# A cross-network kernel: remainder loads re-queued between ScalarE and SyncE, bias copies on ScalarE, one block order

## The chip, the cores and the metric

The kernel runs on one core of a Trainium2 chip. The metric is the device time of one execution in microseconds (us); lower is better. A core has TensorE (PE, matrix products into PSUM), VectorE (DVE), ScalarE (ACT), GpSimd (POOL) and SyncE (SP). SyncE and ScalarE issue DMA transfers here, each on a queue of its own; an engine issues in program order.

## What is computed

Six cross layers (DCN v2) over 4096 rows of 416 features in bf16:

```python
B, F, D, L = 4096, 26, 16, 6          # Din = F * D = 416
def reference(x0, ws, bs):            # x0 [4096, 416], ws [6, 416, 416], bs [6, 416]
    x = x0
    for l in range(ws.shape[0]):
        x = x0 * (x @ ws[l] + bs[l]) + x
    return x
```

## The kernel before

**Layout.** x is kept transposed, features on partitions. The 416 features are three full blocks of 128 (XM, index m for output blocks and k for input blocks) and a remainder of 32. The batch is cut in two halves s = 0 and 1 of 2048 rows, each into four column groups of 512. The four groups of the remainder are stacked on the partitions of one tile XR (group g on partitions 32g to 32g+31), and XRx holds the same with the two 64-partition halves exchanged, so that a matmul can take a group from another row strip of the array. Layers 0 to 4 are computed in this layout; the last layer puts batch rows on partitions and ends in the stores.

**Loads.** Eight transposing DMAs of 512 batch rows each (`load_x0t`, line 77, all from SyncE) bring XM[0]; this text calls them loads 1 to 8. The remainder columns come as plain rows of 64 bytes into `xrem` (`load_xrem`, line 82), in four parts of 64 KB, two for each half of the batch: R0a and R0b (partitions 0:64 and 64:128 of the first half), R1a and R1b (second half). `x0_rem` (line 160) turns a part into XR with VectorE transposes (line 164) and copies (line 165, by ScalarE and VectorE), and then into XRx (line 167, VectorE). For the second half one call handles R1a and R1b together, so it needs both. Layer 0's weights, the biases (`bsb`, line 99) and the remainder rows of the weights (WR, line 100) are issued by ScalarE ahead of everything else.

**Queues before.** SyncE: load 1, load 2, R0a, loads 3 to 6, R1b, loads 7 and 8, then the other layers' weights and the rows of x0 for the last layer. ScalarE: layer 0's weights, biases, WR, three copies of WR rows (line 115), R0b, its share of R0a's copies, R1a. GpSimd: bias columns (lines 105 to 109), three copies of the bias rows to the other partition strips (line 111), then the WD copies (line 136). The bias rows on all strips are first read in the last layer (line 351).

**Layer 0** (`first_layer`, line 239) is written out by hand. TensorE runs warm-up matmuls, then, for the first half: a block of 18 full matmuls (line 246; three output blocks m, two column groups gl, three k each) in PSUM pairs `pa`; six row matmuls (line 254) that add the remainder's part from XR and XRx; a second block of 18 in `pb`; its rows. ScalarE (lines 189 and 172) and VectorE (line 190) take the results out of PSUM. The second half follows with a third block of 18 and its rows. Groups gl = 0 and 1 of the first block read loads 1 and 2, those of the second block loads 3 and 4, those of the third loads 5 and 6. The order of m and gl within a block is a literal list (line 258), which differs between the halves.

**PSUM.** PSUM is used as four pairs of banks, given out by `two_banks` in the order of line 142: the first half's `pa` has pairs 0, 1, 2, its `pb` pairs 3, 0, 2; the second half's `pa` has 1, 3, 0. A pair that is given out again must have been emptied.

Of the kernel before, what the change touches and what calls it, by code (L numbers as in the profile page):

```python
# [16 lines left out]
def kernel(  # L17
# [7 lines left out]
    nc = tc.nc  # L25
# [4 lines left out]
    R = D - NK * P  # L30
    assert R == 32 and B == 4096 and D == 416 and L >= 2
    NS = 2
    NG = 4
# [22 lines left out]
    bsb = const.tile([P, D], BF16)  # L56
# [12 lines left out]
    def col0(s, g):  # L69
        return SW * s + CW * g  # L70
# [4 lines left out]
    def load_x0t(s, g):  # L75
        c0 = col0(s, g)
        nc.sync.dma_start_transpose(out=XM[0][:, :, c0:c0 + CW], in_=x0[c0:c0 + CW, 0:NK * P])


    def load_xrem(eng, s, p0, p1):  # L80
        with nc.allow_non_contiguous_dma(reason="64B row segments"):
            eng.dma_start(xrem[s][p0:p1], x0[SW * s + 16 * p0:SW * s + 16 * p1, NK * P:D].rearrange("(p t) r -> p t r", t=16))
# [24 lines left out]
    for g in range(NG):  # L107
        nc.gpsimd.tensor_copy(bR[32 * g:32 * g + 32, :], bT[:, 4 * NK, 0:L])
    nc.gpsimd.tensor_scalar(out=bR[:, 0:1], in0=bR[:, 0:1], scalar1=1.0, scalar2=None, op0=ALU.add)
    for g in range(1, NG):  # L110
        nc.gpsimd.tensor_copy(bsb[32 * g:32 * g + 32, :], bsb[0:R, :])
    for g in range(1, NG):
        nc.vector.tensor_copy(WR[32 * g:32 * g + 32, 0, :], WR[0:32, 0, :])
    for g in range(1, NG):
        nc.scalar.copy(WR[32 * g:32 * g + 32, 1, :], WR[0:32, 1, :])
    load_x0t(0, 1)
    load_xrem(nc.sync, 0, 0, 64)
    load_xrem(nc.scalar, 0, 64, 128)
    load_x0t(0, 2)
    load_x0t(0, 3)  # L120
    load_x0t(1, 0)
    load_x0t(1, 1)
    load_xrem(nc.sync, 1, 64, 128)
    load_x0t(1, 2)
# [20 lines left out]
    def two_banks():  # L145
        n = turn[0]
        i = first_order[n] if n < len(first_order) else (2, 1, 0, 3)[(n - len(first_order)) % 4]
        turn[0] += 1
        return PS[:, 2 * i:2 * i + 2, :]
# [10 lines left out]
    def x0_rem(s, p0, p1, parts):  # L160
        XRv = XR[0][p0:p1, CW * s:CW * s + CW].rearrange("p (j t) -> p j t", t=16)
        n = 16 // len(parts)
        for a, copy in enumerate(parts):
            nc.vector.transpose(out=xrt[s][p0:p1, n * a:n * a + n, :], in_=xrem[s][p0:p1, n * a:n * a + n, :])  # L164
            copy(XRv[:, :, n * a:n * a + n], xrt[s][p0:p1, n * a:n * a + n, :].rearrange("p t j -> p j t"))
        for a in range(p0, p1, 64):
            nc.vector.tensor_copy(XRx[s][64 - a:128 - a, :], XR[0][a:a + 64, CW * s:CW * s + CW])


    def ew_copy(l, m, pt):  # L170
        t = tpool.tile([P, 2 * CW], BF16, name="t")
        nc.scalar.activation(t[:], pt.rearrange("p a b -> p (a b)"), ACT.Identity, bias=bM[:, m, l:l + 1], scale=1.0)  # L172
        return t[:]

    def ew_main(l, s, m, h, pt, cur, nxt):
        c0 = col0(s, 2 * h)
        t = ew_copy(l, m, pt)
        x0c = XM[0][:, m, c0:c0 + 2 * CW]
        if l == 0:
            nc.vector.tensor_tensor(out=nxt[:, m, c0:c0 + 2 * CW], in0=t, in1=x0c, op=ALU.mult)  # L180
            return
        nc.vector.tensor_tensor(out=t, in0=t, in1=x0c, op=ALU.mult)  # L182
        nc.vector.tensor_tensor(out=nxt[:, m, c0:c0 + 2 * CW], in0=t, in1=cur[:, m, c0:c0 + 2 * CW], op=ALU.add)  # L183


    def split_first(s, m, h, pt, nxt):
        c0 = col0(s, 2 * h)
        t = tpool.tile([P, 2 * CW], BF16, name="t")
        nc.scalar.activation(t[:, 0:CW], pt[:, 0, :], ACT.Identity, bias=bM[:, m, 0:1], scale=1.0)  # L189
        nc.vector.scalar_tensor_tensor(out=nxt[:, m, c0 + CW:c0 + 2 * CW], in0=pt[:, 1, :], scalar=bM[:, m, 0:1],  # L190
                                       in1=XM[0][:, m, c0 + CW:c0 + 2 * CW], op0=ALU.add, op1=ALU.mult)
        return lambda: nc.vector.tensor_tensor(out=nxt[:, m, c0:c0 + CW], in0=t[:, 0:CW], in1=XM[0][:, m, c0:c0 + CW], op=ALU.mult)
# [19 lines left out]
    def mm_row(l, s, m, pts, curR, first, last):  # L212
        for g in range(NG):
            nc.tensor.matmul(pts[g // 2][:, g % 2, :], lhsT=WR[32 * g:32 * g + 32, l, 128 * m:128 * m + 128],  # L214
                             rhs=curR[32 * g:32 * g + 32, CW * s:CW * s + CW],
                             start=first, stop=last, tile_position=(32 * g, 0), skip_group_check=True)
# [11 lines left out]
    def new_pts():  # L228
        return [two_banks() for h in range(2)]
# [9 lines left out]
    def first_layer(s):  # L239
        cur, nxt = XM[0], XM[1]  # L240

        def full(pt, m, h, gl, first, last):
            c0 = col0(s, 2 * h + gl)
            for k in range(NK):
                for q0, q1 in [(32 * q, 32 * q + 32) for q in range(4)] if s == 1 and h == 1 else ((0, P),):
                    nc.tensor.matmul(pt[q0:q1, gl, :], lhsT=WM[:, 0, k, 128 * m + q0:128 * m + q1], rhs=cur[:, k, c0:c0 + CW],  # L246
                                     start=(first and k == 0), stop=(last and k == NK - 1),
                                     tile_position=(0, q0) if s == 1 and h == 1 else None, skip_group_check=True)

        def row(pt, m, h, swapped, first):  # L250
            for gl in range(2):
                r0 = 32 * ((2 * h + gl + 2 * swapped) % 4)
                src = XRx[s][r0:r0 + 32, :] if swapped else XR[0][r0:r0 + 32, CW * s:CW * s + CW]
                nc.tensor.matmul(pt[:, gl, :], lhsT=WR[r0:r0 + 32, 0, 128 * m:128 * m + 128], rhs=src,  # L254
                                 start=first, stop=(not first), tile_position=(r0, 0), skip_group_check=True)

        pa = [two_banks() for m in range(NK)]
        for m, gl in ((0, 0), (1, 0), (2, 0), (0, 1), (1, 1), (2, 1)) if s == 0 else ((0, 0), (1, 0), (0, 1), (1, 1), (2, 0), (2, 1)):
            full(pa[m], m, 0, gl, True, False)
        pb = [two_banks()]  # L260
        row(pa[0], 0, 0, 0, False)
        if s == 1:
            row(pb[0], 0, 1, 0, True)
        row(pa[2], 2, 0, 0, False)
        row(pa[1], 1, 0, 1, False)
        if s == 0:
            closing = [split_first(s, 0, 0, pa[0], nxt)]
            closing.append(split_first(s, 2, 0, pa[2], nxt))
            t1 = ew_copy(0, 1, pa[1])
            for close in closing:  # L270
                close()
            x0_rem(0, 64, 128, (nc.scalar.copy, nc.vector.tensor_copy))
            nc.vector.tensor_tensor(out=nxt[:, 1, 0:2 * CW], in0=t1, in1=XM[0][:, 1, 0:2 * CW], op=ALU.mult)
            pb += [two_banks() for m in range(1, NK)]
            for m, gl in ((0, 0), (1, 0), (2, 0), (0, 1), (1, 1), (2, 1)):
                full(pb[m], m, 1, gl, True, False)
            row(pb[0], 0, 1, 0, False)
            row(pb[1], 1, 1, 0, False)
            row(pb[2], 2, 1, 1, False)
            split_first(s, 0, 1, pb[0], nxt)()  # L280
            x0_rem(1, 0, 128, (nc.vector.tensor_copy,))
            for m in range(1, NK):
                ew_main(0, s, m, 1, pb[m], cur, nxt)
            return None
        split_first(s, 0, 0, pa[0], nxt)()
        for m in (2, 1):
            ew_main(0, s, m, 0, pa[m], cur, nxt)
        full(pb[0], 0, 1, 0, False, False)
        rem_first(0)
        pb += [two_banks() for m in range(1, NK)]  # L290
        full(pb[1], 1, 1, 0, True, False)
        full(pb[0], 0, 1, 1, False, True)
        ew_main(0, s, 0, 1, pb[0], cur, nxt)
        full(pb[1], 1, 1, 1, True, False)
        for gl in range(2):
            full(pb[2], 2, 1, gl, True, False)
        row(pb[1], 1, 1, 0, False)
        row(pb[2], 2, 1, 1, False)
        pt = new_pts()
        mm_row(1, 0, 0, pt, XR[1], True, False)  # L300
        for m in range(1, NK):
            ew_main(0, s, m, 1, pb[m], cur, nxt)
        return pt

    x0_rem(0, 0, 64, (nc.scalar.copy, nc.vector.tensor_copy))
    load_xrem(nc.scalar, 1, 0, 64)

    def rem_pair(l, cur, curR, nxtR, feeds_last):
        pr2 = two_banks()
# [9 lines left out]
    def rem_first(s):  # L319
        pr = two_banks()  # L320
        mm_rem(0, s, pr[:, 0, :], XM[0], XR[0])
        ew_rem(0, s, pr[:, 0, :], XR[0], XR[1])
# [31 lines left out]
    first_layer(0)  # L354
    fill_wd(1, L)
    opened = first_layer(1)


    for l in range(1, LL):
# [6 lines left out]
        def close(t):  # L366
            s, m = t
            for h in range(2):
                ew_main(l, s, m, h, pts[t][h], cur, nxt)
            if feeds_last:  # L370
                xl_dmat(s, m, nxt)
# [116 lines left out]
```

## Time and profile before

| | us |
|---|---|
| median of 3 runs | 130.61 (130.51 to 131.05) |
| the profiled execution | 130.41 |
| its span (first to last instruction) | 128.6 |
| granted TensorE clock, mean | 0.998 |

Busy tenths of the span in 40 slices of 3.2 us, and what the DMA engines did:

```profile
PE   6998999999999999999999999999999999999950
DVE  3358769558697989898989898989898999999990
ACT  2357468693966684966684966584967586676860
POOL 4282000400000000000000000000000050000000
DMA  3999999999970000000000000000599999999563
```

Each digit is the busy share of a slice in tenths. Loads fill the first 37 us; then the DMA engines rest until the last layer. The waits on TensorE by what ended them, in total, times and longest, hold few rows beyond the issue of weights:

```profile
PE PS L153 <- DVE warm L87: 1.0, 1, 1.0
PE PS L246 <- DMA XM<-in_x_dram: 0.5, 2, 0.4
```

The first is the wait for the warm-up's operand at the very start. Matmuls are pipelined, so a gap between the starts of two matmuls that is shorter than one matmul's length does not appear as a wait; such gaps are found by comparing how long equal blocks take.

### The profile page before, as it was taken

How to read it: one execution, taken by the hardware profiler on the slowest of the kernel's cores; microseconds unless marked ns; L12 is line 12 of the kernel's file. 1: busy time of each engine (PE TensorE's matmuls, PEld its weight loads, DVE VectorE, ACT ScalarE, POOL GpSimd, SP SyncE). 2: the span in 40 equal slices, each digit the busy share in tenths (PEclk: the TensorE clock that was granted, in tenths of full speed). 3: DMA queues.
4: the chain of work that ended last, by engine and by line, in shares of the span. 5: the costliest groups of instructions: out<-in, count | busy, mean ns of one | idle time of the engine just before them, and what ended most of it. 6: DMA issues, size and time to landing. Idle time of an engine off the chain costs nothing. (4 is left out here: it accounts for less than half of the span.)

```text
span 128.6 us, 4040 instructions
## 1 busy us (share of the span) xinstructions
PE 122.5 (95%) x1731; PEld 54.9 (43%) x1731; DVE 105.4 (82%) x192; ACT 84.9 (66%) x97; POOL 8.9 (7%) x29
## 2 busy tenths in 40 slices
PE   6998999999999999999999999999999999999950
PEld 3343344444544443554443444443444454454420
DVE  3358769558697989898989898989898999999990
ACT  2357468693966684966684966584967586676860
POOL 4282000400000000000000000000000050000000
PEclk9999999999999999999999999999999999999999
DMA  3999999999970000000000000000599999999563
GB/s 97 259 178 211 189 208 260 262 329 337 333 219 9 3 0 5 0 5 0 5 0 5 0 5 0 0 5 0 54 200 192 123 165 211 77 344 285 178 208 102
DMA packets 41933, 16.28 MB, mean 127 GB/s; under 512 B 30838, under 2 KB 41916, under 8 KB 41916
## 3 DMA queue, kind: packets, MB, share of 16 engines
q1 hardware_dynamic: 39344, 15.53, 55.3%
q10 hardware_dynamic: 2572, 0.51, 2.2%
q8 instruction: 13, 0.21, 0.7%
q14 instruction: 4, 0.03, 0.1%
HBM read 6.07 MB, written 3.41 MB: 74 GB/s over the span
## 5 line engine op out<-in xcount | busy, mean ns | idle before, releaser
L172 ACT ACTIVATE t<-PS,bM 128x1024 bf16<-128x1024 f32 x56 | 58.1, 1114 | 24.0 <-PE PS L214 22.8
L208 PE MATMUL PS<-XM,WM 128*32 128x512 bf16 x1152 | 65.2, 379 | 0.0
L208 PEld LDWEIGHTS <-WM 128*32 128x32 bf16 x1152 | 29.8, 97 | 33.8 <-issue 5.1
L182 DVE TENSOR_TENSOR t<-t,XM 128x1024 bf16<-128x1024 bf16 x48 | 33.2, 691 | 5.4 <-ACT t L172 5.3
L183 DVE TENSOR_TENSOR XM<-t,XM 128x1024 bf16<-128x1024 bf16 x48 | 33.5, 699 | 2.9
L337 PE MATMUL PS<-WM,XM 128*128 128x416 bf16 x96 | 17.9, 340 | 0.0
L246 PE MATMUL PS<-XM,WM 128*32 128x512 bf16 (+1 forms) x126 | 16.6, 379 | 0.6 <-DMA XM<-in_x_dram 0.5
L405 ACT CAST t<-PS 128x832 bf16<-128x832 f32 x12 | 10.1, 854 | 4.2 <-PE PS L337 2.9
L337 PEld LDWEIGHTS <-XM 128*128 128x128 bf16 x96 | 8.9, 98 | 8.6 <-issue 2.1
L246 PEld LDWEIGHTS <-WM 128*32 128x32 bf16 (+1 forms) x126 | 7.2, 97 | 9.6 <-issue 2.6
L225 PE MATMUL PS<-XM,WM 128*32 128x512 bf16 x120 | 8.2, 379 | 0.0
L407 DVE TENSOR_TENSOR o<-t,XLrows 128x832 bf16<-128x832 bf16 x12 | 7.1, 592 | 0.5
L214 PE MATMUL PS<-XR,WR 32*128 32x512 bf16 x96 | 7.5, 379 | 0.0
L406 DVE TENSOR_TENSOR t<-t,X0rows 128x832 bf16<-128x832 bf16 x12 | 7.0, 585 | 0.0
L180 DVE TENSOR_TENSOR XM<-t,XM 128x1024 bf16<-128x1024 bf16 x7 | 4.8, 691 | 2.8 <-ACT t L172 2.7
L316 POOL COPY XLrows<-scrR 128x512 bf16<-128x512 bf16 x2 | 1.6, 809 | 77.3 <-DMA scrR<-XR 77.3
L196 ACT ACTIVATE t<-PS,bR 128x512 bf16<-128x512 f32 x10 | 6.8, 696 | 0.0
L189 ACT ACTIVATE t<-PS,bM 128x512 bf16<-128x512 f32 x4 | 2.6, 685 | 4.7 <-PE PS L254 4.7
L153 PE MATMUL PS<-warm 128*128 128x512 bf16 (+2 forms) x13 | 4.5, 527 | 1.0 <-DVE warm L87 1.0
L418 ACT CAST t<-PS 128x416 bf16<-128x416 f32 x8 | 4.0, 505 | 1.0 <-PE PS L337 0.6
L225 PEld LDWEIGHTS <-WM 128*32 128x32 bf16 x120 | 3.2, 97 | 3.1
L164 DVE STREAM_TRANSPOSE xrt<-xrem 64x256 bf16<-64x256 bf16 (+1 forms) x5 | 2.2, 477 | 2.3 <-DMA xrem<-in_x_dram 2.3
(45 smaller groups left out, 55.3 us busy)
## 6 DMA issues: line engine op xcount, KB each, us to landing
X0rows<-in_x_dram SPq DMA_DIRECT2D x6, 416.0 KB, 7.7
WM<-in_ws_dram SPq DMA_DIRECT2D x5, 312.0 KB, 5.5
out_dram<-o SPq DMA_DIRECT2D x3, 416.0 KB, 4.3
out_dram<-o SPq DMA_DIRECT2D x6, 208.0 KB, 2.1
X0rows<-in_x_dram SPq DMA_DIRECT2D x1, 832.0 KB, 9.6
out_dram<-o SPq DMA_DIRECT2D x8, 104.0 KB, 1.7
WR<-in_ws_dram SPq DMA_DIRECT2D x4, 104.0 KB, 4.8
WM<-in_ws_dram ACTq DMA_DIRECT2D x1, 312.0 KB, 3.4
```

Of the source, the lines that this page charges most:

```text
L172: nc.scalar.activation(t[:], pt.rearrange("p a b -> p (a b)"), ACT.Identity, bias=bM[:, m, l:l + 1], scale=1.0)
L182: nc.vector.tensor_tensor(out=t, in0=t, in1=x0c, op=ALU.mult)
L183: nc.vector.tensor_tensor(out=nxt[:, m, c0:c0 + 2 * CW], in0=t, in1=cur[:, m, c0:c0 + 2 * CW], op=ALU.add)
L196: nc.scalar.activation(tr[:, 0:CW], pr, ACT.Identity, bias=bR[:, l:l + 1], scale=1.0)
L208: nc.tensor.matmul(pts[g // 2][32 * q:32 * q + 32, g % 2, :], lhsT=WM[:, l, k, 128 * m + 32 * q:128 * m + 32 * q + 32], rhs=cur[:, k, c0:c ...
L214: nc.tensor.matmul(pts[g // 2][:, g % 2, :], lhsT=WR[32 * g:32 * g + 32, l, 128 * m:128 * m + 128], rhs=curR[32 * g:32 * g + 32, CW * s:CW ...
L225: nc.tensor.matmul(pr[32 * g:32 * g + 32, :], lhsT=WM[:, l, k, NK * P:D], rhs=cur[:, k, c0:c0 + CW], start=False, stop=(k == NK - 1), tile ...
L246: nc.tensor.matmul(pt[q0:q1, gl, :], lhsT=WM[:, 0, k, 128 * m + q0:128 * m + q1], rhs=cur[:, k, c0:c0 + CW], start=(first and k == 0), sto ...
L337: nc.tensor.matmul(py[g // 2][:, g % 2, 0:D], lhsT=xL[:, k, q_cols(q, g)], rhs=WM[:, LL, k, :], start=(first and k == 0), stop=((not first ...
L405: nc.scalar.copy(tv, py[h][:, :, 0:D])
L406: nc.vector.tensor_tensor(out=tv, in0=tv, in1=X0rows[:, b0:b0 + 5:4, :], op=ALU.mult)
L407: nc.vector.tensor_tensor(out=o, in0=tv, in1=XLrows[:, b0:b0 + 5:4, :], op=ALU.add)
```

## The change

Four things are moved.

- R0a is issued by ScalarE in place of SyncE, right behind a ScalarE copy of bias rows that waits for the biases to land. R0b, R1a and R1b are all issued by SyncE, behind loads 4, 5 and 6. R0b and R1a were ScalarE's before; R1b keeps its place behind load 6.
- Two of the three copies of the bias rows go from GpSimd to ScalarE, the third stays.
- The second half's block in layer 0 takes the order of the first half's: all three m of the first column group, then those of the second.
- R1a's issue at the end of the first `x0_rem` call goes away (it is now on SyncE).

```diff
@@ -107,18 +107,20 @@
     for g in range(NG):
         nc.gpsimd.tensor_copy(bR[32 * g:32 * g + 32, :], bT[:, 4 * NK, 0:L])
     nc.gpsimd.tensor_scalar(out=bR[:, 0:1], in0=bR[:, 0:1], scalar1=1.0, scalar2=None, op0=ALU.add)
-    for g in range(1, NG):
-        nc.gpsimd.tensor_copy(bsb[32 * g:32 * g + 32, :], bsb[0:R, :])
+    nc.scalar.copy(bsb[32:64, :], bsb[0:R, :])
+    load_xrem(nc.scalar, 0, 0, 64)
+    nc.scalar.copy(bsb[64:96, :], bsb[0:R, :])
+    nc.gpsimd.tensor_copy(bsb[96:128, :], bsb[0:R, :])
     for g in range(1, NG):
         nc.vector.tensor_copy(WR[32 * g:32 * g + 32, 0, :], WR[0:32, 0, :])
     for g in range(1, NG):
         nc.scalar.copy(WR[32 * g:32 * g + 32, 1, :], WR[0:32, 1, :])
     load_x0t(0, 1)
-    load_xrem(nc.sync, 0, 0, 64)
-    load_xrem(nc.scalar, 0, 64, 128)
     load_x0t(0, 2)
     load_x0t(0, 3)
+    load_xrem(nc.sync, 0, 64, 128)
     load_x0t(1, 0)
+    load_xrem(nc.sync, 1, 0, 64)
     load_x0t(1, 1)
     load_xrem(nc.sync, 1, 64, 128)
     load_x0t(1, 2)
@@ -255,7 +257,7 @@
         pa = [two_banks() for m in range(NK)]
-        for m, gl in ((0, 0), (1, 0), (2, 0), (0, 1), (1, 1), (2, 1)) if s == 0 else ((0, 0), (1, 0), (0, 1), (1, 1), (2, 0), (2, 1)):
+        for m, gl in ((0, 0), (1, 0), (2, 0), (0, 1), (1, 1), (2, 1)):
             full(pa[m], m, 0, gl, True, False)
@@ -303,7 +305,6 @@
     x0_rem(0, 0, 64, (nc.scalar.copy, nc.vector.tensor_copy))
-    load_xrem(nc.scalar, 1, 0, 64)
```

Line numbers in the profile of the kernel before are its own; in the changed kernel lines 122 to 305 stand two further on, and those behind 306 one.

## The prediction

> **What bounds the kernel now.** I read the page's busy table first, then busy time by stage, then the timeline of the first 22 us, then the rows of single loads. Loads 1 to 8 are the eight transposing x0 loads in SyncE's order; R0a, R0b, R1a, R1b are the four remainder parts (first or second half of the batch, partitions 0:64 or 64:128).
>
> ```profile
> PE 122.5 (95%) x1731; PEld 54.9 (43%) x1731; DVE 105.4 (82%) x192; ACT 84.9 (66%) x97; POOL 8.9 (7%) x29
> ```
>
> ```profile
> 5.00:10.00 5.00, 4.83 (x27) 1.93 (x24) 2.81 (x8) 2.23 (x4) 3.88 (x14) 1.00 1.13 201
> 10.00:15.00 5.00, 4.61 (x28) 1.92 (x25) 4.21 (x9) 2.89 (x4) 0.64 (x4) 1.00 1.23 209
> 15.00:20.00 5.00, 5.00 (x36) 1.84 (x35) 3.63 (x8) 2.79 (x4) 0.00 (x0) 1.00 1.16 208
> ```
>
> The columns of the second view are the stretch, its length, busy time of PE, PEld, DVE, ACT and POOL, granted TensorE clock, DMA share and GB/s. TensorE bounds the kernel: from 15 us on every stretch up to 120 us is full at clock 1.00, so whatever the first 20 us lose or win stays in the end time one for one. What can be won is only in the first 15 us. The timeline shows where:
>
> ```profile
> 4.82 0.60 DVE L103 STREAM_TRANSPOSE bT<-bsb 32x416 bf16<-32x416 bf16 x1 [2.86 <-DMA bsb<-in_bs_dram]
> 4.93 0.66 SPq L82 DMA_DIRECT2D xrem<-in_x_dram  x1
> 5.64 7.66 SPq L77 DMA_TRANSPOSE XM<-in_x_dram  x4
> 5.71 4.05 PE L246 MATMUL PS<-XM,WM 128*128 128x512 bf16 x18 [0.17 <-DMA XM<-in_x_dram]
> ...
> 5.95 0.54 ACT L115 COPY WR<-WR 32x416 bf16<-32x416 bf16 x1 [2.07 <-DMA WR<-in_ws_dram]
> 5.96 0.63 ACTq L82 DMA_DIRECT2D xrem<-in_x_dram  x1
> ...
> 8.17 0.76 DVE L164 STREAM_TRANSPOSE xrt<-xrem 64x256 bf16<-64x256 bf16 x2 [1.38 <-DMA xrem<-in_x_dram]
> 8.97 0.40 DVE L165 COPY XR<-xrt 64x256 bf16<-64x256 bf16 x1
> 9.47 0.45 DVE L167 COPY XRx<-XR 64x512 bf16<-64x512 bf16 x1
> 9.69 0.60 PE L254 MATMUL PS<-XR,WR 32*128 32x512 bf16 x4
> 9.97 0.39 PE L254 MATMUL PS<-XRx,WR 32*128 32x512 bf16 x2
> 10.73 4.23 PE L246 MATMUL PS<-XM,WM 128*128 128x512 bf16 x18 [0.37 <-DMA XM<-in_x_dram]
> 13.61 0.29 DVE L167 COPY XRx<-XR 64x512 bf16<-64x512 bf16 x1
> 15.43 4.06 PE L246 MATMUL PS<-XM,WM 128*128 128x512 bf16 x18
> 15.90 2.11 ACT L172 ACTIVATE t<-PS,bM 128x1024 bf16<-128x1024 f32 x2
> 18.73 0.61 DVE L167 COPY XRx<-XR 64x512 bf16<-64x512 bf16 x2
> 19.66 0.38 PE L254 MATMUL PS<-XRx,WR 32*128 32x512 bf16 x2
> ```
>
> Eighteen full matmuls take 4.05 us at one every 0.216 ((4.05 - 0.38)/17, the last one's own length being 0.38). Load 3, issued at 5.64 and landed 5.0 later (its row), is what the block at 10.73 waits for. Rows to block is normally 0.31 (15.12 to 15.43), so without that wait the block starts at 9.97 + 0.31 = 10.28: 0.45 lost. The block takes 4.23 instead of 4.05: its tenth matmul waits for load 4 (issued 7.8 + 5.0 = 12.8), 0.18 lost. Together 0.63 us, the most that better loads can win. The R0a chain is level with TensorE as it is: it lands at 4.93 + 3.2 = 8.13, its last copy (9.47, 0.45) ends at 9.92, and the matmul that reads XRx starts at 9.97.
>
> **The change part by part.**
>
> Loads 3 and 4 lose the R0a issue (0.66) ahead of them: issued 0.7 earlier, landing by 5.0 each at 9.93 and about 12.1. Load 3 is then early (needed at 10.28 or later), load 4 too (needed at 10.28 + 9 x 0.216 = 12.22). Gain: up to 0.45 and 0.18.
>
> R0a moves to ScalarE. The bias copy put ahead of it waits for the biases, which are there when DVE L103 starts, 4.82. Before, ScalarE's issue at 5.96 came 0.01 after the first of three queued copies began, so an issue does not wait for the copy's end: R0a is issued at about 4.85, 0.08 earlier than before. But these two rows disagree on how long such a load takes:
>
> ```profile
> L82 SPq DMA_DIRECT2D xrem<-in_x_dram x1: 655/655/655, 4.9 to 4.9; - x1
> ...
> DMA to landing us min/median/max: 3.2/3.2/3.2
> ```
>
> ```profile
> L82 ACTq DMA_DIRECT2D xrem<-in_x_dram x1: 634/634/634, 6.0 to 6.0; - x1
> ...
> DMA to landing us min/median/max: 4.5/4.5/4.5
> ```
>
> From SyncE 3.2 (and 3.9 for R1b at 13.34), from ScalarE 4.5, for the same 64 KB. ScalarE's other part, R1a at 8.65, has no landing row, but its queue (q10 in the packet view) carries its last packets in the stretch 11.5 to 12, some 3.2 after issue, where R0b's came in 9.5 to 10, some 3.8 after: about 0.6 better, so I estimate 4.0 for it. Bounds 3.2 and 4.5; I take 4.25, the middle of ScalarE's two, since R0a will likewise run beside a transposing load just issued. R0a then lands at 9.10, and the chain starts 0.97 later than before (8.13). One thing shortens the chain: the XRx copy took 0.45 while GpSimd was copying bias rows, and 0.29 for the same shape at 13.61 with GpSimd idle. Two of GpSimd's bias copies (0.57 each of 1.72) are gone and its WD copies move ahead, so 0.16 less. The XRx rows start at 9.97 + 0.97 - 0.16 = 10.78, the next block 0.31 later at 11.09, 0.36 after the present 10.73. Load 4's wait is gone, -0.18. Sum for the first half: +0.18.
>
> A rule of the Trainium skill speaks against this step's cost: DMA: Bandwidth & Descriptors, section "Issuing engines are not separate DMA queues", says that transfers started by any engine run on the same 16 DMA engines and interleave, so that another issuer saves only the issue time. By it R0a would take 3.2 as on SyncE; this trace has 4.5 beside 3.2, though under different neighbours. It stands as the first rival.
>
> The block order of the second half changes: its third group of three matmuls is now m=2 instead of the second column group. That tile's PSUM pair is the one that m=1 of the first half's second block used, and the first of the two ACT L172 at 15.90 (1.11 each) empties it, till 17.01. TensorE reaches the group after six matmuls, 15.43 + 6 x 0.216 = 16.73, and must wait until about 17.05: +0.32. Before, it came 12 matmuls in (18.0). ScalarE's copy waits itself for the matmuls just ahead, so the wait moves along with any shift. What the new order covers: load 6 lands now at 11.39 + 5.2 = 16.6, just ahead of 16.73. It is issued up to 0.65 later (two remainder issues ahead of it on SyncE instead of one), so lands by 17.2; its first use moves to 15.43 + 9 x 0.216 + 0.32 = 17.7. No second cost.
>
> R0b, behind load 4: issue at 8.5 to 9.2, landing 3.2 to 3.9 later, 11.7 to 13.1. DVE takes it at 12.32, in my sum 0.6 later; its rows are read at 14.89, a chain of 1.6 behind: nothing. R1a behind load 5 is needed together with R1b. R1b, behind load 6, has 0.65 more issue work ahead: landing 17.25 to 17.9, so the last XRx copy ends between 19.34 and 19.99, against the rows that read it at 19.66 plus my shift of 0.5: nothing. Loads 7, 8 and layer 1's weights are up to 0.65 later; the weights (issued 17.98, 5.5 to land, so 23.5 to 24.1) are read at 25.5: nothing. ScalarE's two bias copies (0.54 each) lie in its 2.07 us wait before 5.95; without that cover they would delay its WR copies by 1.1.
>
> Sum: +0.36 - 0.18 + 0.32 = +0.50 us. The profiled execution took 130.41 (span 128.6 and 1.8 around it), so 130.9 for one like it; the median of the three runs is 130.61, so 131.1.
>
> **The rivals.**
> 1. R0a lands from ScalarE as fast as from SyncE (3.2: at 8.05). Then both load waits vanish, the order's 0.32 stays: -0.63 + 0.32 = -0.31, 130.3. For it: the 4.5 was of a load issued with both R0a and load 3 under way, and R0a will have only the tail of load 2 ahead of it. Against: the 4.5 row. It wins from a landing before about 8.6, where the sum is zero. Chance 0.18.
> 2. R0a is later still, because the issue waits for the bias copy's 0.54 or because load 3, now issued with it, takes the DMA engines first: chain 1.51 late, +0.90 - 0.18 + 0.32 = +1.04, 131.65. Against the first reason: the 0.01 between copy and issue above. Chance 0.20. The first reason would also be the change not doing what it says.
> 3. The order's wait does not come (ScalarE empties the pair in time): +0.18, 130.8. Against: 17.01 stands against 16.73, and both follow the same rows. Chance 0.09.
> 4. SyncE's longer queue decides: R1b's full 0.65 makes XRx ready 19.99 instead of just before 19.66, +0.38, 131.0, if R0a comes early enough. Chance 0.08.
> My forecast, +0.35 to +0.75: 0.45.
>
> **How the numbers follow.** 0.5% is 0.65 us, about what a measurement of this kernel tells from no change. Slower than that: all of rival 2 and four tenths of the forecast, 0.38. Faster than that needs rivals 1 and 3 together (-0.63) and a little more: 0.06. Within: 0.56. The range runs from rival 1 to rival 2, 130.3 to 131.7.
>
> **What would show it.** In the changed trace: ScalarE's remainder issue at about 4.85 and its landing row (4.0 to 4.5 for me, 3.2 for rival 1); DVE's first transpose of xrem at about 9.1; no DMA wait at the second block, which takes 4.05, not 4.23; in the third block a gap of some 0.3 after six matmuls, ended by ACT L174 (the L172 of now); XRx rows of the second half not waiting. I am wrong if R0a lands before 8.6, if the third block takes 4.06 without a gap, or if new TensorE gaps appear past 22 us.

## The result, and the profile after

The changed kernel takes 131.08 us (median of 22 runs, 130.53 to 131.87), the one before beside it 130.59 (22 runs, 130.18 to 131.08): a ratio of 1.0044, 95% interval 1.0028 to 1.0060, so 0.4 to 0.8 us slower. Its profiled execution took 131.03 with a span of 129.2, against 130.41 and 128.6.

TensorE's own timeline of the changed kernel in layer 0 (start, length, what; in brackets the idle time before it and what ended that):

```profile
5.57 4.04 PE L248 MATMUL PS<-XM,WM 128*128 128x512 bf16 x18 [0.18 <-DMA XM<-in_x_dram]
9.55 0.39 PE L256 MATMUL PS<-XR,WR 32*128 32x512 bf16 x2
9.63 0.39 PE L256 MATMUL PS<-XRx,WR 32*128 32x512 bf16 x2
...
10.09 4.09 PE L248 MATMUL PS<-XM,WM 128*128 128x512 bf16 x18
...
14.64 1.47 PE L248 MATMUL PS<-XM,WM 128*128 128x512 bf16 x6
16.27 2.86 PE L248 MATMUL PS<-XM,WM 128*128 128x512 bf16 x12 [0.16 <-ACT t L174]
19.74 0.61 PE L256 MATMUL PS<-XR,WR 32*128 32x512 bf16 x6 [0.61 <-DVE XR L167]
20.06 0.39 PE L256 MATMUL PS<-XRx,WR 32*128 32x512 bf16 x2
20.45 0.83 PE L248 MATMUL PS<-XM,WM 128*32 128x512 bf16 x12
```

Two things happened that the sum did not have. The second block starts at 10.09 straight behind its rows, and no longer waits for a load: the first half won time. And the second half's rows, which waited for nothing before, start at 19.74 after an idle stretch of 0.61 that ends with VectorE's copy into XR. The gap after six matmuls of the third block, ended by ScalarE, is there: 14.64 + 6 x 0.216 = 15.94 against 16.27, 0.33.

The same stretch from the side of the loads, first R0a on ScalarE's queue and two of VectorE's three takings of `xrem` (R0a's and the second half's), then SyncE's queue:

```profile
4.61 0.64 ACTq L82 DMA_DIRECT2D xrem<-in_x_dram  x1
...
8.00 0.76 DVE L166 STREAM_TRANSPOSE xrt<-xrem 64x256 bf16<-64x256 bf16 x2 [1.35 <-DMA xrem<-in_x_dram]
...
18.35 0.71 DVE L166 STREAM_TRANSPOSE xrt<-xrem 128x512 bf16<-128x512 bf16 x1 [2.43 <-DMA xrem<-in_x_dram]
```

```profile
9.46 2.78 SPq L77 DMA_TRANSPOSE XM<-in_x_dram  x1
12.29 0.59 SPq L82 DMA_DIRECT2D xrem<-in_x_dram  x1
12.92 1.80 SPq L77 DMA_TRANSPOSE XM<-in_x_dram  x1
14.77 0.59 SPq L82 DMA_DIRECT2D xrem<-in_x_dram  x1
15.40 3.98 SPq L77 DMA_TRANSPOSE XM<-in_x_dram  x2
19.42 0.58 SPq L73 DMA_DIRECT2D WM<-in_ws_dram  x1
```

R0a is issued as the bias copy begins and VectorE takes it at 8.00 (before: 8.17). R1b is issued at 14.77 instead of 13.34, 1.43 later, and taken at 18.35 instead of 17.35. Layer 1's weights are issued at 19.42 instead of 17.98.

The page's row of GB/s (40 slices of 3.2 us), before and after:

```profile
GB/s 97 259 178 211 189 208 260 262 329 337 333 219 9 3 0 5 0 5 0 5 0 5 0 5 0 0 5 0 54 200 192 123 165 211 77 344 285 178 208 102
```

```profile
GB/s 96 267 198 167 174 150 218 240 317 329 333 331 56 3 0 5 0 5 0 5 0 5 0 5 0 0 5 0 46 202 197 133 170 200 103 348 255 178 199 104
```

Slices 4 to 6, 9.6 to 19.2 us, fall from 211, 189, 208 to 167, 174, 150 with the DMA engines at eight or nine tenths in both: that is where R0b, R1a and R1b follow each other on SyncE's queue.

| moment (us) | before | after | after, second profile |
|---|---|---|---|
| first block starts | 5.71 | 5.57 | 5.50 |
| second block | 10.73 | 10.09 | 10.07 |
| third block | 15.43 | 14.64 | 14.63 |
| rows of the second half | 19.42 | 19.74 | 19.47 |
| block behind them | 19.96 | 20.45 | 20.11 |
| layer 1's first full matmul | 25.54 | 26.05 | 25.58 |
| span | 128.6 | 129.2 | 128.7 |

So 0.79 was won by 14.64 (0.14 of it is an earlier start of the first block) and more than that lost by 20.45. The second profile is that of the last run, the changed kernel once more.

### The profile page after: what moved, and what is told of

The parts are those of the page before. It is cut to its first block, busy times and chain, and to the rows that moved or that the text cites. A ratio compares the mean times of both kernels' runs of the same rounds, so it can differ in the third digit from the quotient of the medians.

```text
span 129.2 us, 4040 instructions
## 1 busy us (share of the span) xinstructions
PE 122.5 (95%) x1731; PEld 55.2 (43%) x1731; DVE 104.9 (81%) x192; ACT 86.1 (67%) x99; POOL 8.4 (7%) x27
```

## The experiments

All edits are to the changed kernel. Ratios are to the kernel before on the same chip, with their 95% intervals. Two things were to be told apart: what R0a's and the other parts' queues are worth, and whether the new order or R1b costs the second half.

**The old order back.**

```diff
-        for m, gl in ((0, 0), (1, 0), (2, 0), (0, 1), (1, 1), (2, 1)):
+        for m, gl in ((0, 0), (1, 0), (2, 0), (0, 1), (1, 1), (2, 1)) if s == 0 else ((0, 0), (1, 0), (0, 1), (1, 1), (2, 0), (2, 1)):
```

> The changed kernel with the second half's block back in its old order; everything else as changed. Theory A (the landing of R1b, 18.25 in the changed kernel, decides when the second half's rows start, so the order is free): the wait for PSUM goes (0.32), load 6, landed at 16.98, is now wanted at 15.94 and takes about 1.0 in its place, the rows still start at about 19.7; 131.1 within 0.15. Theory B (the order's wait is a loss of its own): 130.75.

131.19, ratio 1.0044 (1.0023 to 1.0066): theory A. TensorE's timeline of this run:

```profile
14.80 1.47 PE L248 MATMUL PS<-XM,WM 128*128 128x512 bf16 x6
16.94 2.75 PE L248 MATMUL PS<-XM,WM 128*128 128x512 bf16 x12 [0.67 <-DMA XM<-in_x_dram]
19.66 0.61 PE L256 MATMUL PS<-XR,WR 32*128 32x512 bf16 x6
```

The wait for PSUM is replaced by one for load 6 at the same place (0.84 beyond the 16.10 that six matmuls would give), and the rows start at 19.66. Two things end together here: load 6's wait alone would put the rows at 19.63 (16.94 and 12 matmuls at the pace before), and VectorE's copy of R1b's rows into XR ends at 19.61. So the order is worth nothing: without PSUM's wait, load 6 and R1b hold the rows at the same place.

**R0a back on SyncE, ahead of load 3.**

```diff
-    load_xrem(nc.scalar, 0, 0, 64)
...
+    load_xrem(nc.sync, 0, 0, 64)
     load_x0t(0, 2)
```

> The changed kernel with R0a back on SyncE ahead of load 3; R0b, R1a, R1b stay behind loads 4, 5, 6 on SyncE. Theory A (each part on SyncE's queue holds up what is behind it by 0.65 of issue and some 0.7 more): the waits for loads 3 and 4 return (0.6) and R1b lands another 0.7 to 1.4 later, rows of the second half at 20.4 to 21.1; 131.8 to 132.5. Theory B (where R0a is issued does not matter, all run on the same engines): 131.1.

132.47, ratio 1.0151 (1.0124 to 1.0179), at the upper end of theory A in time, but not by A's way. In its profile SyncE issues R1b 0.51 later than in the changed kernel's and layer 1's weights only 0.07 later (19.49 against 19.42). The second block does not wait for a load, the rows of the second half start at 19.95, and the last matmul starts only 0.3 later than in the changed kernel's first profile (124.53 against 124.26) and 0.7 later than in its second. Another 0.8 of the span lies behind the last matmul, where SyncE waits for the last stores to land (1.4 at the longest, 0.4 in the changed kernel). So R0a's place on ScalarE is worth something, yet how much of the 1.4 us belongs to it and why the end is slower was not settled. The profile also points to what else the first half's gain hangs on. Load 3 is issued at 5.53, nearly as late as in the kernel before (5.64), yet it lands at 9.56 instead of 10.69, ahead of its use, now that R0b is no longer issued beside it. Load 3 took 5.05 and 5.56 from issue to landing in the two kernels that issue both R0a and R0b by 6 us (the kernel before, and the run with all parts on ScalarE below), and 4.0 to 4.9 in the other twelve profiles.

**R1a and R1b on ScalarE.** Issued behind ScalarE's first remainder copy, where R1a was before.

```diff
-    load_xrem(nc.sync, 1, 0, 64)
-    load_xrem(nc.sync, 1, 64, 128)
...
     x0_rem(0, 0, 64, (nc.scalar.copy, nc.vector.tensor_copy))
+    load_xrem(nc.scalar, 1, 0, 64)
+    load_xrem(nc.scalar, 1, 64, 128)
```

> The changed kernel with R1a and R1b issued by ScalarE behind the first remainder copy (where R1a was before), so SyncE carries only R0b between loads. Theory A: R1b lands by 14, loads 6 to 8 are about 1.3 earlier, the rows of the second half no longer wait (0.68 less) and load 6 neither (0.11 less); only PSUM's wait of 0.32 is left; 130.2 to 130.4. Theory B (on ScalarE's queue they hold up the transposing loads just as much): 130.9 to 131.2.

130.47, ratio 1.0008 (0.9982 to 1.0034): the loss is gone, though not the 0.2 to 0.4 below the kernel before that A asked for. TensorE and VectorE:

```profile
15.44 4.04 PE L246 MATMUL PS<-XM,WM 128*128 128x512 bf16 x18 [0.27 <-DMA XM<-in_x_dram]
19.41 0.60 PE L254 MATMUL PS<-XR,WR 32*128 32x512 bf16 x6
```

```profile
16.36 0.70 DVE L164 STREAM_TRANSPOSE xrt<-xrem 128x512 bf16<-128x512 bf16 x1
```

The remainder is taken at 16.36, with no wait, and the rows go straight on. But the third block now waits for load 5, which took 5.7 from its issue instead of the changed kernel's 4.6: the two parts ran beside it. The first half's gain was paid back there.

**All four parts on ScalarE, old order.** R0b behind ScalarE's WR copies, R1a and R1b as in the run before.

> R0a as changed; R0b on ScalarE behind its WR copies, R1a and R1b on ScalarE behind the first remainder copy; the old order in the second half. SyncE issues nothing but the eight loads. Theory A: load 6 is issued at about 10.5 and lands by 15.6, ahead of its first use at 15.94, so neither a load nor PSUM is waited for; 129.9 to 130.1. Theory B (parts on ScalarE's queue hold up the loads as much): load 6 lands at 16.5 or later and costs 0.5 or more; 130.5 to 130.8.

130.57, ratio 0.9996 (0.9979 to 1.0012): B's range in time, but neither theory as stated. SyncE issues layer 1's weights at 17.38 (17.98 in the kernel before), and the rows of the second half wait for nothing. What took the gain in the profile are two other things. Its first eight full matmuls took 2.52 instead of 1.89 (the last section). And ScalarE's issue of R1b was held: the two issues span 2.03 where 0.54 each is their length, the second starting at 10.54, 0.02 behind the landing of load 3, whose semaphore it uses (a wait that is met again further down). ScalarE's copy out of PSUM stands behind them, until TensorE waits for it:

```profile
11.93 3.40 PE L246 MATMUL PS<-XM,WM 128*128 128x512 bf16 x15 [0.22 <-ACT t L189]
```

**One part more on SyncE; one part more on ScalarE.** The same 64 KB into a tile that nothing reads, ahead of R1b on SyncE in the one, at about 8.5 on ScalarE in the other.

```diff
+    load_xrem(nc.sync, 1, 0, 64, xtra)
     load_xrem(nc.sync, 1, 64, 128)
```

> The changed kernel with one load more of R1a's size (64 KB in 64-byte pieces, into a tile that nothing reads) on SyncE between load 6 and R1b. Theory A (a remainder part costs SyncE's queue some 1.3 us of its DMA engines, and R1b's landing sets the second half): R1b lands about 1.3 later, rows of the second half at about 21.0; 132.2 to 132.5. Theory B, the prediction's price (a part costs what follows its issue time only, 0.65): 131.7.

> The changed kernel with the same additional load on ScalarE instead, behind its first remainder copy (issue at about 8.5). Theory A (the DMA engines are full, so a part costs time on either queue, less on ScalarE's where it runs beside the loads): R1b lands 0.5 to 1.0 later; 131.5 to 132.0. Theory B (a part beside the loads is free): 131.1. Theory C (the same as on SyncE): 132.2 to 132.5.

On SyncE 132.77, ratio 1.0162 (1.0137 to 1.0187); on ScalarE 131.07, ratio 1.0046 (1.0028 to 1.0065), beside 1.0044 without it. The rows of the second half and SyncE's queue, first with the part on SyncE:

```profile
21.42 0.40 PE L258 MATMUL PS<-XR,WR 32*128 32x512 bf16 x4 [1.79 <-DVE XR L169]
```

```profile
13.22 2.39 SPq L78 DMA_TRANSPOSE XM<-in_x_dram  x1
15.66 0.59 SPq L83 DMA_DIRECT2D xtra<-in_x_dram  x1
16.29 0.67 SPq L83 DMA_DIRECT2D xrem<-in_x_dram  x1
17.00 3.83 SPq L78 DMA_TRANSPOSE XM<-in_x_dram  x2
20.88 0.58 SPq L74 DMA_DIRECT2D WM<-in_ws_dram  x1
```

then with it on ScalarE:

```profile
20.41 0.60 PE L257 MATMUL PS<-XR,WR 32*128 32x512 bf16 x6 [0.94 <-DVE XR L168]
```

```profile
19.85 0.58 SPq L74 DMA_DIRECT2D WM<-in_ws_dram  x1
```

With the part on SyncE the time is about 1.5 longer (1.0162 against 1.0044) and the last matmul 1.48 later (125.74 against 124.26), over twice the 0.59 that the part's issue takes: theory B, the prediction's price, is refuted as a price in time. But the profile does not show the part holding its queue for 1.5. Load 6's issue (13.22, 2.39 long) ends at 15.61, ahead of the part, where the changed kernel's ends at 14.72: 0.89 of the 1.52 by which R1b is issued later stands there already, and the part itself adds 0.63. With one profile, whether the 0.89 belongs to the edit or to that execution is not known.

With the part on ScalarE layer 1's weights are issued 0.43 later, R1b lands 0.68 later and the rows start 0.67 later, as A said, while the time is B's: A's lowest, 131.5, is 1.0070 of the 130.59 that it was reckoned from, just beyond the interval. C is out. The two runs differ in more than the queue: the part is issued at 15.66, right ahead of R1b, in the one, and at 8.56 in the other.

**R0a on ScalarE a microsecond later**, behind the first WR copy.

```diff
-    load_xrem(nc.scalar, 0, 0, 64)
...
         nc.scalar.copy(WR[32 * g:32 * g + 32, 1, :], WR[0:32, 1, :])
+        if g == 1:
+            load_xrem(nc.scalar, 0, 0, 64)
```

> The changed kernel with R0a issued by ScalarE behind its first WR copy (about 5.85, a microsecond behind the issue of load 3) instead of behind the bias copy (4.61). Theory A (what counts is whether the part is issued ahead of load 3 or behind it; behind it takes 4.5 as R0b did before): R0a lands at about 10.3, the first half loses 1.9, of which the second half's wait for R1b takes back some 0.7; 132.2 to 132.6. Theory B (3.4 wherever it is issued): landing at 9.25; 131.3 to 131.6.

133.9, ratio 1.0259 (1.0237 to 1.0282). R0a's rows and TensorE:

```profile
L82 ACTq DMA_DIRECT2D xrem<-in_x_dram x1: 625/625/625, 5.8 to 5.8; - x1
...
DMA to landing us min/median/max: 4.5/4.5/4.5
```

```profile
11.66 0.61 PE L257 MATMUL PS<-XR,WR 32*128 32x512 bf16 x4 [1.98 <-DVE XR L168]
...
12.28 5.74 PE L249 MATMUL PS<-XM,WM 128*128 128x512 bf16 x17
```

The landing is A's to the tenth: 4.5 behind load 3's issue, 3.4 ahead of it, on the same queue. The time went 1.3 beyond A, because the next block took 5.74 instead of 4.1 (the last section).

**R1a and R1b as one load, old order.**

```diff
-    load_xrem(nc.sync, 1, 0, 64)
...
-    load_xrem(nc.sync, 1, 64, 128)
+    load_xrem(nc.sync, 1, 0, 128)
```

> The changed kernel with R1a and R1b as one load of 128 KB behind load 6 on SyncE, and the old order in the second half. Theory A (with one part less ahead of it load 6 lands at about 15.6, ahead of its first use at 15.94, so neither it nor PSUM is waited for; the one load is cheaper than two, R1 lands at 17.5 to 17.8 in place of 18.25): rows of the second half at 19.0 to 19.3; 130.2 to 130.5. Theory B (no gain from one load in place of two, R1 at 18.25 or later): 131.1.

131.2, ratio 1.0047 (1.0019 to 1.0076): theory B. VectorE takes R1 at 18.42 and the rows start at 19.81. SyncE issues layer 1's weights at 19.42, just as with two loads, so joining the two issues frees nothing; that it is the 128 KB in 64-byte pieces that cost is argued from this, not shown.

**Looking for a version that beats both.** R1 as one load on ScalarE behind its copy of m=1 (new and old order), and R0b on ScalarE too:

```diff
             t1 = ew_copy(0, 1, pa[1])
+            load_xrem(nc.scalar, 1, 0, 128)
```

> The changed kernel with R1a and R1b as one load of 128 KB on ScalarE, behind its copy of the first block's m=1 (issue at about 11.2), so that SyncE carries R0b alone between its loads; new order. Theory A (a part on ScalarE's queue runs beside the loads and costs them little): loads 3 to 5 as in the changed kernel, load 6 by 16.6, R1 by 16.5; the second half's rows wait for nothing, PSUM's 0.32 is all that is left of the loss; 130.0 to 130.3. Theory B (it holds up load 6 as on SyncE): load 6 at 17.3 or later; 130.7 to 131.

> The same with the old order in the second half. Theory A: PSUM's 0.32 is gone but load 6 is wanted at 15.94 and lands at 16.0 to 16.6; 129.9 to 130.4. Theory B: load 6 at 17.3, 1.3 lost there; 130.8 to 131.2.

> As the run before, and R0b on ScalarE too, behind the first remainder copy (issue at about 8.5): SyncE issues the eight loads and nothing else, and no issue of ScalarE waits for an earlier transfer. Theory A: load 6 is issued at about 10.5 and lands by 15.9, R0b at 12.9, R1 by 16.5; neither loads nor PSUM are waited for; 129.8 to 130.1. Theory B (the DMA engines are full and the order of the queues changes nothing in sum): 130.5 or more.

130.84 (ratio 1.0012, 0.9997 to 1.0028), 130.73 (1.0015, 0.9999 to 1.0030) and 131.64 (1.0105, 1.0064 to 1.0147). None beats the kernel before, and A missed all three. In the first the issue fell at 10.44, in the middle of load 5's, and load 5 took 6.4 to land; the third block paid for it:

```profile
16.01 4.05 PE L246 MATMUL PS<-XM,WM 128*128 128x512 bf16 x18 [1.13 <-DMA XM<-in_x_dram]
```

In the last, an issue on ScalarE did wait, against what its expectation said: R1's goes out only at 14.73, when load 5 (issued 9.2, 5.5 to land) is in. In the trace the transfers share eight semaphores, and an issue that uses one again waits for that semaphore: R1's had been load 5's. ScalarE's remainder copy stood behind it, and TensorE waited 1.22 for that. (This profile is of the slowest of the six executions, 133.22.)

**The changed kernel once more.**

> The changed kernel once more beside the three above: 131.1 (1.0044 of the kernel before). In its profile, whatever the start of the first block: R0a 3.3 to 4.1 after issue, a gap of 0.3 at the third block's seventh matmul, rows of the second half waiting for XR some 0.7, R1b landing 1.0 later than in the kernel before.

131.02, ratio 1.0030 (1.0010 to 1.0051). R0a landed 3.4 after issue, and TensorE's timeline has the same two gaps:

```profile
16.26 2.76 PE L248 MATMUL PS<-XM,WM 128*128 128x512 bf16 x12 [0.16 <-ACT t L174]
19.47 0.61 PE L256 MATMUL PS<-XR,WR 32*128 32x512 bf16 x6 [0.45 <-DVE XR L167]
```

The rows wait a little less (0.52 beyond their normal place instead of 0.68). VectorE takes R1b at 18.08, 0.73 later than in the kernel before, not the 1.0 expected.

**All profiles side by side.** When SyncE issues layer 1's weights, by the number of 64 KB remainder parts on its queue ahead of them (the 128 KB load counted as two):

| parts on SyncE's queue | profiles | layer 1's weights issued (us) |
|---|---|---|
| none | all on ScalarE, as three loads and as four | 17.20, 17.38 |
| one | R1 on ScalarE, three versions | 17.88, 17.97, 18.10 |
| two | the kernel before | 17.98 |
| three | the changed kernel twice, four edits of it | 19.21, 19.35, 19.41, 19.42, 19.42, 19.85 |
| four | R0a on SyncE; one part more on SyncE | 19.49, 20.88 |

The 19.85 is that of the run with one part more on ScalarE. From none (17.3) to three (19.4) a part moves the queue by 0.7 on average, little more than its own issue. The steps are uneven, though: hardly anything between one and two, 1.2 at the least between two and three, and 1.4 between the two versions with four.

## Why the total was right and its terms were not

The sum said +0.50 and 131.1; the median is 131.08. That agreement is a coincidence of two wrong terms, one of each sign.

- **R0a's landing, "+0.36": wrong.** The step that failed is the choice of 4.25 us from the one ScalarE row. It measured 3.4 here, and 3.3 to 4.1 in the eleven profiles that issue R0a behind the bias copy, always less than 4.25; the second block came 0.64 earlier (0.14 of it the first block's start), not 0.36 later. R0b's 4.5 was put down to ScalarE's queue; the late R0a shows that it belonged to being issued behind load 3 (4.5 again). The first rival was right, and so was, for this part, the rule of the Trainium skill beside it (DMA: Bandwidth & Descriptors, "Issuing engines are not separate DMA queues"): 3.4 on ScalarE against 3.2 on SyncE. The gain itself needs more than R0a's place: with R0a back on SyncE load 3 also landed in time (9.56), with R0b no longer issued beside it.
- **Load 4's wait, -0.18: right but for its size.** The second block takes 4.09 instead of 4.23, so 0.14 was won; the 0.04 over 4.05 falls on the first matmul that writes to PSUM's pair 0 again.
- **XRx copy, -0.16: right in size.** It takes 0.28 (0.45 before), though GpSimd is not idle beside it but copies WD, and the XRx rows now start with the first rows.
- **The order's wait for PSUM, +0.32: right**, 0.33 in both profiles. But it decides nothing: with the old order the time is the same.
- **Load 6, "no second cost": nearly.** TensorE waits 0.11 for it (2.86 for twelve matmuls against 2.75), since it gets there earlier than in the sum.
- **R1b, "nothing": wrong, and the largest error.** The step was "0.65 more issue work". R1b's issue comes 1.43 later, and the rows lose 0.68 behind all other waits. Of the 1.43, the second part ahead of R1b makes 0.64 with its gaps, as the prediction had it; what it left out is that the issues of loads 3 to 6 themselves got longer, 8.45 in all instead of 7.53, or 0.92 (the queue's start 0.13 earlier takes the rest off). Why they got longer is open. An R1b that decides is the fourth rival's mechanism, here with a larger price. The "nothing" also leaned on the first half's forecast shift of 0.5, which would have hidden a late R1b and did not come. Here the rule of the Trainium skill cited in the first item, that another issuer saves only the issue time, is not settled: taking R1a and R1b off the queue brought layer 1's weights forward by 1.32 (19.42 to 18.10), 0.66 each, which fits it; the added part cost 1.5 us of kernel time on SyncE's queue and none that could be measured on ScalarE's, which does not, but the moments of issue differed too.
- **Layer 1's weights, "nothing": not in every execution.** In the profile after they took 6.6 from issue to landing, and TensorE waited for them, 0.19 beyond the normal step (a row of the waits: engine, line, releaser, total, times, longest):

```profile
PEld L210 <- DMA WM<-in_ws_dram: 0.6, 1, 0.6
```

In the second profile they took 3.8 and nothing waited. In the kernel before they landed at 22.48, 4.5 from issue (the prediction's 5.5 is the median of five such loads), and were read at 25.54, so a spread of that size lay hidden; issued 1.44 later, it no longer does.

From the first table: -0.79 to the third block, +0.33 for PSUM, +0.11 for load 6 and +0.68 for XR give +0.33 at the rows (0.32 measured). Then +0.17 up to the next block, where the last XRx copy and load 7 come late, -0.17 of slack up to layer 1, and +0.19 for the weights: +0.51 at 26.05, kept to the end of the span.

The two large errors are linked. Once the first half is early, R1b's copy alone sets the rows, at 19.74; had R0a landed as forecast, the rows would by the sum start at 19.92, later than that, and the end would hardly differ.

That R1a and R1b on SyncE's queue cost the loss is shown by taking them off it: the ratio falls from 1.0044 to 1.0008, and to 1.0012 and 1.0015 with the two joined (the changed kernel beside these: 1.0030, with an interval that overlaps theirs). That a fourth part there costs 1.4 to 1.5 of time is shown by two runs (R0a, and the added part), but their profiles do not agree on where. What lengthens SyncE's issues, and whether a part is dearer there than on ScalarE's queue at the same moment, is open. The bandwidth row falls where the parts follow each other on one queue, which suits parts whose small pieces run alone instead of beside a transposing load; that is argued only. The first half's gain is shown by both profiles of the changed kernel, in which the second block does not wait for a load; its size in the end time was not measured by itself.

## What to carry to other kernels

Do not price a transfer that is put into a queue by its own issue alone: see in the trace how much later everything behind it is issued, and whether the issues around it got longer. Add one such transfer and take the time of many executions and more than one profile, since the delay in one profile can stand ahead of what was added. A landing time read from one row belongs to its neighbours in time as much as to its queue: look at what was issued just ahead of it. When a sum comes out right, compare the terms with the trace before believing any of them.

## What the runs showed of the hardware

A pause of TensorE can cost more than itself. In the run with the late R0a, TensorE was idle for 1.98 us, and from 12.6 to 15.9 matmuls then started every 0.427 us instead of 0.216. Stretch, length, busy times of PE, PEld, DVE, ACT and POOL, granted clock, DMA share, GB/s:

```profile
11.00:12.00 1.00, 0.34 (x6) 0.18 (x6) 0.77 (x3) 0.43 (x1) 0.00 (x0) 1.00 0.77 97
...
13.00:14.00 1.00, 1.00 (x4) 0.39 (x3) 1.00 (x3) 1.00 (x2) 0.00 (x0) 0.50 0.79 116
14.00:15.00 1.00, 1.00 (x4) 0.37 (x3) 0.97 (x3) 0.65 (x2) 0.00 (x0) 0.50 1.22 127
```

The granted clock fell to 0.50. A pause of 1.79 in the run with the part added on SyncE did not do that. The Trainium skill (TensorE: Matmul & The Clock Gate, "Part 1: The HAM clock gate") gives an idle window of about 3.4 us for the fall to half rate; this run fell after less, and the measurement decides. The 3.4 us of work that the page gives for the return to full rate agree with the 3.3 that the slow stretch lasted here.

The end of the warm-up phase moves between executions of like kernels: full matmuls ran at 0.216 apart from the first one in the kernel before, but only from about 7 us in the run with all parts on ScalarE, which cost it 0.63. Such a shift is as large as the effect studied here; a single profile's span does not rank these kernels.
